# Attention sums of the first units out of the value products, key copies ahead of maxima, and first weight packs rounded on GpSimd

## The chip, the cores and the metric

The kernel runs on one core of a Trainium2 chip. The core has five engines with a queue each: TensorE (PE: matmuls, with weight loads listed apart as PEld), VectorE (DVE), ScalarE (ACT), GpSimd (POOL) and SyncE (SP), which here issues every DMA. Each engine runs its queue in program order and waits on semaphores for the others. The metric is the time of one execution in device microseconds (us), as the median of several runs; a profile shows one execution.

## The reference

Two stages, all in float32. First an attention over 4 batches of 8 heads, 768 positions and 64 numbers per head, in which a query sees the keys less than 16 positions away and 24 block summaries:

```python
k_sum = k.reshape(B, H, nb, 32, D).max(axis=3)
v_sum = v.reshape(B, H, nb, 32, D).mean(axis=3)
scores_l = np.where(|i - j| < 16, scale * q @ k.T, -1e9)
scores_s = scale * q @ k_sum.T + log(32)
a = exp(scores_all - max); a = a / (sum(a) + 1e-9)
attn = a @ concat(v, v_sum)
```

Then, on the 3072 rows x of 512 numbers that this gives: `out = ((x @ w_a) * (x @ w_b)) @ w_out`, with 1536 columns in the middle.

## The kernel before

**Work is cut in units.** A unit is 256 rows (two tiles of 128 queries), so there are 12. Per unit the second stage runs 12 items, one per 128 middle columns: 144 items. An item is 24 matmuls for `x @ w_a` and `x @ w_b` (line 959), a product on DVE (L979) between copies on ACT (L976, L981), a rest on DVE (L984) and 6 matmuls onto the output (L995). Float32 accuracy is had by parts: x and the weights are split into a rounded part and a rest, and three products are added. The split of x is a cast on ACT (L747) and a subtraction on DVE (L750).

**Weights** come in 36 loads (`load_part`, L255), two to a *pack*; `convert(j)` makes the parts of pack j = 0 to 17 by bit operations: scaling on ACT into PSUM bank c0 (L294), four steps on DVE (`step`, L309 to L333, with c1 between; three steps from pack 2 on, where ACT also writes the signs, L294 to S), then a rounding cast on ACT (L369) and a subtraction and an addition on POOL (L374, L380). Packs 0, 1 and 14 to 17 go in halves of 512 columns, the others in one piece of 1024. Loads of packs from 4 on wait for the pack four places earlier.

**Attention.** `first_keys` turns the six key chunks of batch 0 on PE (`turn`, L401), copies each out in two pieces on ACT (L460, L462) and takes block maxima on DVE (L470); POOL puts the summaries between the keys (L436). `first_attention` does units 0 and 1 (`u < FILL`), tiles 0 to 3, in this chain: the mask is laid into two PSUM banks by a matmul (L598), the queries are turned and scaled, the scores are added (L610), maxima on DVE (L643), exponentials on ACT with an accumulated sum (L655), then 1e-9 added, a reciprocal and a diagonal matrix of it on DVE (L664, L670, L677), a matmul of the exponentials with the diagonal that transposes and divides at once (L698), a copy on ACT (L710), the products with the values (L739) with the heads' dimensions on partitions, and the split of x. The means of the value blocks come from matmuls with `mean` (L852), copies on ACT (L864) and POOL (L870). Tiles 0 and 2 share buffers and banks o0, o1; tiles 1 and 3 share o2, o3. Later units (`attention`) divide on POOL (L685) and transpose on DVE (L725). Unit 2's two tiles use banks c0 and c1, which the conversion uses too: the second tile's scores stand behind pack 17's last use of them.

**The order** is planned by the class `Work`: every operation is added with an engine, a rank, an estimated duration and the keys that it reads and writes; `emit` then lets each engine take the operation with the lowest rank among those that the plan has ready. The ranks that matter here: CHAIN 0 for an item's copies and the scaling, FIRST 1 for unit 0 and keys, NEXT 2.3 for unit 1, CONVERT 2 + j/4 for pack j on DVE (0.5 less for its cast), SOON 5 for unit 2. The items of units 0 and 1 alternate, so that each new weight serves two items; from unit 2 on all weights are there.

Of the kernel before, what the change touches and what calls it, by code (L numbers as in the profile page):

```python
# [84 lines left out]
def attention_moe(  # L85
# [27 lines left out]
    SIGNS = 2  # L113
    AHEAD = (7, 9, 17)
# [64 lines left out]
    vbuf = [sb([P, H, D], f"vw{e}") for e in range(2)]  # L179
    for e in range(2):  # L180
        nc.vector.memset(vbuf[e], 0.0)
# [48 lines left out]
    CHAIN, FIRST, CONVERT, NEXT, SOON, PREP, LATER = 0, 1, 2, 2.3, 5, 5.5, 6  # L230
# [40 lines left out]
    def convert(j):  # L271
# [81 lines left out]
        for hs in spans:  # L353
# [13 lines left out]
            act(  # L367
                rank - 0.5, 0.25 + 0.37 * len(hs), f + rk, hi,
                lambda ms=ms, f8=f8: nc.scalar.copy(out=parted(0)[:, ms], in_=f8),  # L369
            )  # L370
# [73 lines left out]
    def first_keys():  # L444
        n = P // BLK
        for i in range(S // P):
# [7 lines left out]
            pe(FIRST, 0.85, [key], [bk], lambda bk=bk, x=x: turn(bank[bk], x))  # L454
            c0 = PER * i

            def put(lo, bk=bk, c0=c0):
                tr = bank[bk].rearrange("p (c x) -> p c x", x=P)
                if lo:
                    nc.scalar.copy(out=kT[:, :, c0 + 16 : c0 + WIN], in_=tr[:, :, : WIN - 16])  # L460
                else:
                    nc.scalar.copy(  # L462
                        out=kT[:, :, c0 + P : c0 + PER + 16], in_=tr[:, :, WIN - 16 :]
                    )
# [11 lines left out]
        for c in range(NP):  # L476
            work.add("-", 0, 0, 0, [f"ksi{i}" for i in range(6)], [f"ks{c}"], lambda: None)
            reads = [f"kT{x}{i}" for i in range(6) for x in "lh"]
            work.add("-", 0, 0, 0, reads, [f"kT{c}k"], lambda: None)
            summaries(FIRST, c)  # L480
# [93 lines left out]
    def load_values(b, t, vw, keys, rank):  # L574
# [3 lines left out]
        for i, (e, r0, lo, hi) in enumerate((  # L578
# [5 lines left out]
                rank, 2.1 * (hi - lo), 215, (), [keys[i]], vw[e][r0 : r0 + hi - lo],  # L584
# [3 lines left out]
    def scores(u, t, qT, qk, s, sk, banks, diag=None, lead=None):  # L588
        kind = 0 if t == 0 else 2 if t == S // P - 1 else 1
        rank = rank_of(u) + (0.2 * (t % G) if u < FILL else 0)  # L590
        m, mk = nml[t % 2], f"nml{t % 2}"


        masked = u < FILL

        def masks():
            for h in range(2):
                nc.tensor.matmul(  # L598
                    bank[banks[h]].rearrange("p (c x) -> p c x", x=P), ident,
                    mask[:, kind, None, :].broadcast_to([P, NP, P]), start=True, stop=False,  # L600
                )

        def fn():
            for c in range(NP):
                for h in range(2):
                    hs = slice(h * D, (h + 1) * D)
                    for e in range(2):
                        es = slice(e * QT, (e + 1) * QT)
                        c0 = PER * t + QT * e
                        nc.tensor.matmul(  # L610
                            bank[banks[h]][es, c * P : (c + 1) * P], qT[hs, c, es],
                            kT[hs, c, c0 : c0 + P],
                            start=not masked, stop=not masked or c == NP - 1,
                            tile_position=(h * D, e * QT),
                        )

        if masked:
            pe(rank + 0.1, 1.8, [], banks, masks)
        if lead is None:
            pe(-1, 1.2, [qk] + KT, banks, fn)  # L620
        else:

            def both():
                lead[2]()
                fn()

            pe(-1, 2.2, lead[0] + [qk] + KT, [lead[1], *banks], both)
# [446 lines left out]
```

## Time and profile before

| what | us |
|---|---|
| median of 3 runs | 705.59 (703.9 to 707.14) |
| the profiled execution, whole | 703.89 |
| its span from the first to the last instruction | 702.2 |
| mean granted clock of TensorE | 0.995 |

Lines of a page or view name an engine, a kernel line (L), what is written and read, and a count (x). An entry in brackets is the idle time of the engine before the instruction and what ended it. A timeline's first two columns are start and duration in us, and neighbours of one kind are merged into a row.

### The profile page before, as it was taken

To read this page: it belongs to the slowest core of one execution; us is meant where nothing else is said; L and a number is where in the kernel's file an instruction comes from. 1 tells how busy PE (TensorE), PEld (TensorE's weight loads), DVE (VectorE), ACT (ScalarE), POOL (GpSimd) and SP (SyncE) were. 2 spreads that over 40 slices of the span, in tenths; PEclk is the share of its full clock that TensorE was granted. 3 is DMA by queue.
4 is the path that set the end of the run, shared out by engine and by line. 5 is a ranking of instruction groups with operands and counts; after the bars stand their busy time and mean duration, and the time that the engine had idled before them with its cause. 6 is when DMAs were issued, how large, how long until landed. Compare 5 with 4: busy or idle time off the path is not lost.

```text
span 702.2 us, 15117 instructions
## 1 busy us (share of the span) xinstructions
PE 682.5 (97%) x6000; PEld 626.5 (89%) x6000; DVE 439.8 (63%) x992; ACT 271.2 (39%) x815; POOL 182.3 (26%) x220
## 2 busy tenths in 40 slices
PE   6889999999999999999999999999999999999997
PEld 3768998898999999999999999999999999999996
DVE  2899899897767777767665776762762662311221
ACT  2998787532424332333332323332331431211211
POOL 5269878652442440113110101110110110000000
PEclk9989999999999999999999999999999999999999
DMA  9989835165224245132210330310310100000000
GB/s 227 280 182 291 301 80 155 27 141 125 64 74 98 70 99 116 32 58 78 54 24 17 69 67 2 87 24 1 84 24 1 54 21 1 31 1 1 31 1 31
DMA packets 154943, 54.84 MB, mean 78 GB/s; under 512 B 132456, under 2 KB 147816, under 8 KB 154872
## 3 DMA queue, kind: packets, MB, share of 16 engines
q1 hardware_dynamic: 154872, 53.88, 32.0%
q8 instruction: 47, 0.77, 0.5%
q14 instruction: 24, 0.20, 0.1%
HBM read 47.12 MB, written 6.29 MB: 76 GB/s over the span
## 4 chain that ended last, share of the span: by engine, by line
PE 85%; DVE 7%; ACT 4%; DMA 2%; issue 1%; POOL 0%; SPq 0%; POOLq 0%; DVEq 0%; ACTq 0%
PE h L959 51%; PE o L995 27%; PE c L739 2%; PE c L610 2%; PE o L739 2%; DVE pt L725 1%; DMA raw<-in_moe_w_b_dram 1%; PE o L610 1%; ACT s L655 1%; DVE c L327 1%; ACT c L294 1%; ACT S L294 1%; DVE ksum L470 1%; PE o L598 1%; DVE gl L984 0%
## 5 line engine op out<-in xcount | busy, mean ns | idle before, releaser
L959 PEld LDWEIGHTS h<-x,w 128*128 128x128 f32 x3456 | 413.9, 188 | 10.8 <-DVE c L327 0.2
L959 PE MATMUL h<-x,w 128*128 128x256 f32 x3456 | 416.3, 277 | 0.0
L979 DVE TENSOR_TENSOR h<-h,g 128x256 f32<-128x256 f32 x144 | 62.0, 430 | 163.7 <-ACT g L976 162.4
L976 ACT COPY g<-h 128x256 f32<-128x256 f32 x144 | 53.7, 373 | 277.6 <-PE h L959 276.8
L995 PE MATMUL o<-w,gh 128*128 128x512 f32 x576 | 158.0, 396 | 1.9 <-ACT gh L981 1.9
L995 PEld LDWEIGHTS o<-w,gh 128*128 128x128 f32 x576 | 98.8, 188 | 19.5 <-ACT gh L981 2.7
L725 DVE STREAM_TRANSPOSE pt<-s 32x256 f32<-32x256 f32 x240 | 104.7, 436 | 8.3 <-POOL s L685 4.0
L685 POOL TENSOR_TENSOR s<-s,nml 128x512 f32<-128x512 f32 x40 | 41.7, 1042 | 243.1 <-DVE nml L670 241.5
L995 PE MATMUL o<-w,gl 128*128 128x512 f32 x288 | 89.7, 393 | 0.0
L655 ACT ACTIVATE s<-s,nml 128x128 f32<-128x128 f32 x160 | 62.5, 393 | 49.5 <-DVE nml L643 46.8
L984 DVE TENSOR_TENSOR gl<-h,gh 128x256 fp32r<-128x256 f32 x144 | 60.5, 420 | 29.7 <-ACT gh L981 28.2
L981 ACT CAST gh<-h 128x256 fp32r<-128x256 f32 x144 | 53.5, 372 | 62.9 <-DVE h L979 62.6
L995 PEld LDWEIGHTS o<-w,gl 128*128 128x128 f32 x288 | 53.9, 188 | 11.7
L540 POOL TENSOR_TENSOR S<-S 96x512 f32<-96x512 f32 (+3 forms) x48 | 33.5, 698 | 49.6 <-DMA S<-in_v_dram 39.8
L655 ACT ACTIVATION_READ_ACCUMULATOR s<-s,nml 128x1 f32 x160 | 30.3, 190 | 0.0
L664 DVE TENSOR_SCALAR nml<-nml 128x4 f32<-128x4 f32 x40 | 11.5, 287 | 30.0 <-ACT s L655 30.0
L374 POOL TENSOR_TENSOR space<-space,w 128x1024 f32<-128x1024 f32 (+1 forms) x13 | 26.8, 2058 | 11.8 <-ACT w L369 10.9
L380 POOL TENSOR_TENSOR w<-space 128x1024 fp32r<-128x1024 f32 (+1 forms) x13 | 26.8, 2064 | 1.0
L294 ACT ACTIVATE S<-raw 128x1024 f16<-128x1024 f32 (+1 forms) x20 | 23.1, 1153 | 6.5 <-DVE S L309 4.6
L643 DVE TENSOR_REDUCE nml<-s 128x4 f32<-128x512 f32 x40 | 25.2, 667 | 0.0
L294 ACT ACTIVATE c<-raw 128x512 f32<-128x512 f32 x36 | 23.2, 645 | 4.0 <-DVE space L320 1.5
L436 POOL COPY kT<-ksum 128x144 f32<-128x144 f32 x16 | 4.7, 307 | 61.0 <-DVE ksum L518 55.0
(104 smaller groups left out, 478.0 us busy)
## 6 DMA issues: line engine op xcount, KB each, us to landing
raw<-in_moe_w_a_dram SPq DMA_DIRECT2D x12, 512.0 KB
raw<-in_moe_w_b_dram SPq DMA_DIRECT2D x12, 512.0 KB
raw<-in_moe_w_out_dram SPq DMA_DIRECT2D x12, 512.0 KB
out_dram<-S SPq DMA_DIRECT2D x24, 256.0 KB
qin<-in_q_dram SPq DMA_DIRECT2D x160, 32.0 KB
S<-in_v_dram SPq DMA_DIRECT2D x24, 192.0 KB
vw<-in_v_dram SPq DMA_DIRECT2D x18, 192.0 KB
kin<-in_k_dram SPq DMA_DIRECT2D x24, 100.0 KB
```

The lines of the kernel that those rows point to most:

```text
L294: nc.scalar.mul(out=zhalf[:, lo:hi] if out is None else out, in_=high.bitcast(F32), mul=2.0**-112)
L540: lambda: nc.gpsimd.tensor_tensor(out=out, in0=i0, in1=i1, op=ALU.add),
L655: lambda h=h, c=c, sums=sums: nc.scalar.activation(s[h][:, c, :], x[h][:, c, :], AF.Exp, bias=m[:, 0, h, c : c + 1], scale=1.0, accum_out= ...
L685: lambda h=h, r=r: nc.gpsimd.tensor_tensor(out=s[h], in0=s[h], in1=r[:, :, None].broadcast_to([P, NP, P]), op=ALU.mult,),
L725: lambda js=js, qs=qs: nc.vector.transpose(out=pv[js, :, qs], in_=sv[qs, :, js]),
L739: nc.tensor.matmul(ps[h * D : (h + 1) * D, c, es], vw[e][:, 2 * c + h, :], d[:, h, c, es], start=True, stop=True, tile_position=(0, h * D),)
L959: nc.tensor.matmul(ps, w[:, c, part, :], x[xpart][:, c, :], start=(i == 0), stop=(i == n - 1))
L976: act(CHAIN, 0.38, [hk], [gk], lambda: nc.scalar.copy(out=g, in_=pa))
L979: lambda: nc.vector.tensor_tensor(out=pa, in0=pb, in1=g, op=ALU.mult),
L981: act(CHAIN, 0.41, [hk], [ghk], lambda: nc.scalar.copy(out=gh, in_=pa))
L984: lambda: nc.vector.tensor_tensor(out=gl, in0=pa, in1=gh.bitcast(F32), op=ALU.subtract),
L995: nc.tensor.matmul(bank[ok[j]], (gh if first else gl)[:, js], w[:, :, part, :], start=(f == 0 and first and part == 0), stop=(f == NF - 1 ...
```

## The change

Four things change together.

1. In units 0 and 1 the sums of the exponentials come out of the value products. The value buffers get a 65th column of ones per head, and the products are formed with the queries on partitions (`weigh`), so that column 64 holds the sum. The exponentials have no accumulator, they are transposed by the identity, the division comes after the products, and the result is turned back on PE. The second set of value buffers moves in part to the upper half of S1.
2. The halves of the value rows for the block means are added on POOL, and one mean matmul per chunk is left instead of two.
3. In `first_keys` both copies stand ahead of the maximum, which waits for them. The mask matmuls wait for the first key turn and are one per bank.
4. Packs 0 to 3 are rounded by POOL instead of ACT (`FIRSTS = 4`). NEXT goes from 2.3 to 1.5, and the first two weight loads from ranks 8 and 9 to 5 and 5.5, ahead of unit 0's queries (6 and 7).

For units 2 to 11 the same operations are written in other functions.

```diff
+    vbuf = [sb([P, H, D + 1], f"vw{e}") for e in range(2)]
     for e in range(2):
-        nc.vector.memset(vbuf[e], 0.0)
+        nc.vector.memset(vbuf[e][:, :, :D], 0.0)
+        nc.vector.memset(vbuf[e][:, :, D:], 1.0)
...
-    CHAIN, FIRST, CONVERT, NEXT, SOON, PREP, LATER = 0, 1, 2, 2.3, 5, 5.5, 6
+    CHAIN, FIRST, CONVERT, NEXT, SOON, PREP, LATER = 0, 1, 2, 1.5, 5, 5.5, 6
...
+            if j < FIRSTS:
+                pool(
+                    rank - 0.5, 0.1 + 0.55 * len(hs), f + rk, hi,
+                    lambda ms=ms, f8=f8: nc.gpsimd.tensor_copy(out=parted(0)[:, ms], in_=f8),
+                )
+            else:
...
-            act(FIRST, 0.43, [bk], [f"kTl{i}"], lambda put=put: put(True))
-            act(FIRST, 0.33, [bk], [f"kTh{i}"], lambda put=put: put(False))
+            act(FIRST, 0.75, [bk], [f"kT{i}"], put)
             dve(
-                FIRST, 0.6, [bk], [f"ksi{i}"],
+                FIRST, 0.6, [bk, f"kT{i}"], [f"ksi{i}"],
...
+    def early_scores(u, t, qT, qk, s, sk, banks):
...
+        for h in range(2):
+            pe(
+                rank + 0.1, 0.9, ["first"], [banks[h]],
+                lambda h=h: nc.tensor.matmul(
+                    x[h], ident, mask[:, kind, None, :].broadcast_to([P, NP, P]),
+                    start=True, stop=False,
+                ),
+            )
+        pe(-1, 1.2, [*qk] + KT, banks, lambda: dots(t, qT, banks, False))
...
+                act(
+                    rank, 0.2, [f"{mk}m{h}", banks[h]], [sk[h]],
+                    lambda h=h, c=c: nc.scalar.activation(
+                        s[h][:, c, :], x[h][:, c, :], AF.Exp, bias=m[:, 0, h, c : c + 1]
+                    ),
+                )
...
+    def early_values(u, t, s, sk, banks, pt, vw, vk):
...
+        def turned(h):
+            for c in range(NP):
+                nc.tensor.transpose(bank[banks[h]][:, c * P : (c + 1) * P], s[h][:, c, :], ident)
...
+        def weigh(j):
+            for i in range(NP):
+                g = NP * j + i
+                for e in range(2):
+                    es = slice(e * QT, (e + 1) * QT)
+                    nc.tensor.matmul(
+                        ps[j][es, i, :], d[:, g % 2, g // 2, es], vw[e][:, g, :],
+                        start=True, stop=True, tile_position=(0, e * QT),
+                    )
+
+        for j in range(2):
+            pe(-1, 0.55, dk[0] + dk[1] + vk, [banks[j]], lambda j=j: weigh(j))
+        for j in range(2):
+            l = m[:, 1, j, :]
+            dve(
+                rank, 0.15, [banks[j]], [f"{mk}l"],
+                lambda j=j, l=l: nc.vector.tensor_scalar(
+                    out=l, in0=ps[j][:, :, D], scalar1=1e-9, scalar2=None, op0=ALU.add
+                ),
+            )
+            dve(rank, 0.15, [], [f"{mk}l"], lambda l=l: nc.vector.reciprocal(out=l, in_=l))
+            dve(
+                rank, 0.4, [banks[j], f"{mk}l"], [sk[0]],
+                lambda j=j, l=l: nc.vector.tensor_tensor(
+                    out=xn[:, j * 256 : (j + 1) * 256].rearrange("p (g d) -> p g d", d=D),
+                    in0=ps[j][:, :, :D], in1=l[:, :, None].broadcast_to([P, NP, D]), op=ALU.mult,
+                ),
+            )
+        pe(-1, 0.6, [sk[0]], [banks[1]], lambda: turn(bank[banks[1]], xn))
+        split(u, t, banks[1])
...
+            pool(
+                FIRST, 0.7, [], [key],
+                lambda x=x: nc.gpsimd.tensor_tensor(
+                    out=x[:, :, :D], in0=x[:, :, :D], in1=x[:, :, D:], op=ALU.add
+                ),
+            )
+            pe(FIRST + 0.5, 0.5, [key, mk], ["h0"], lambda n=n: means(n))
...
-    for i, rank in enumerate((8, 9, 17, 17.5, 19, 20)):
+    for i, rank in enumerate((5, 5.5, 17, 17.5, 19, 20)):
```

More of the change, by code (lines that the diff above doesn't have):

```diff
@@ L477, in first_keys @@
             work.add("-", 0, 0, 0, [f"ksi{i}" for i in range(6)], [f"ks{c}"], lambda: None)
-            reads = [f"kT{x}{i}" for i in range(6) for x in "lh"]
-            work.add("-", 0, 0, 0, reads, [f"kT{c}k"], lambda: None)
+            work.add("-", 0, 0, 0, [f"kT{i}" for i in range(6)], [f"kT{c}k"], lambda: None)
             summaries(FIRST, c)
@@ L583, in load_values, with scores @@
             load(
-                rank, 2.1 * (hi - lo), 215, (), [keys[i]], vw[e][r0 : r0 + hi - lo],
+                rank, 2.1 * (hi - lo), 215, (), [keys[i]], vw[e][r0 : r0 + hi - lo, :, :D],
                 heads(v[b, :, lo:hi, :]),
             )
-    def scores(u, t, qT, qk, s, sk, banks, diag=None, lead=None):
+    def scores(u, t, lead=None):
         kind = 0 if t == 0 else 2 if t == S // P - 1 else 1
-        rank = rank_of(u) + (0.2 * (t % G) if u < FILL else 0)
+        rank = rank_of(u)
         m, mk = nml[t % 2], f"nml{t % 2}"
[L594 to L618, printed above, removed]
+        banks = ["c0", "c1"] if u == FILL or t % G == 0 else ["o2", "o3"]
         if lead is None:
-            pe(-1, 1.2, [qk] + KT, banks, fn)
+            pe(-1, 1.2, ["qT"] + KT, banks, lambda: dots(t, qTs, banks, True))
         else:
@@ L691, in transposes @@
[L691 to L714 removed]
+                rank, 0.15, [], lk,
@@ new lines, in scores @@
+                lambda l=l: nc.vector.tensor_scalar(
+                    out=l, in0=l, scalar1=1e-9, scalar2=None, op0=ALU.add
+                ),
+            )
+            dve(rank, 0.15, [], lk, lambda l=l: nc.vector.reciprocal(out=l, in_=l))
+            pool(
+                rank, 1.05, lk, [SK[h]],
+                lambda h=h, l=l: nc.gpsimd.tensor_tensor(
+                    out=s0[h], in0=s0[h], in1=l[:, :, None].broadcast_to([P, NP, P]), op=ALU.mult
+                ),
+            )
@@ L730, in products, with split @@
+    def split(u, t, bk):
         rank = rank_of(u)
         ps = bank[bk].rearrange("p (c x) -> p c x", x=P)
-        d, dk = pt or PD
+        hi, lo = (y[:, :, P * (t % G) : P * (t % G + 1)] for y in xs[u % 2])
+        xk = f"x{u % 2}.{t % G}"
+        act(rank, 0.6, [bk], [xk + "h"], lambda: nc.scalar.copy(out=hi, in_=ps))
+        dve(
+            rank, 0.6, [bk, xk + "h"], [xk + "l"],
+            lambda: nc.vector.tensor_tensor(out=lo, in0=ps, in1=hi.bitcast(F32), op=ALU.subtract),
+        )
@@ L734, in fn, with products @@
+    def products(u, t, bk):
+        ps = bank[bk].rearrange("p (c x) -> p c x", x=P)
         def fn():
@@ L924, in attention @@
             begin(0)
-            turned(0)
+            transposes(u)
             yield
@@ L943, in attention @@
                 bring(i)
-                turned(i)
+                transposes(u)
                 lead.append(products(*end(i)))
         if u == NU - 1:
-            reads, bk, fn, split = lead.pop()
+            reads, bk, fn, then = lead.pop()
             pe(-1, 1.1, reads, [bk], fn)
-            split()
+            then()
         yield
```

244 lines of the change are left out of this document (114 added, 130 removed).

## The prediction

> **What bounds the kernel now.** The page comes first: its busy line.
>
> ```profile
> PE 682.5 (97%) x6000; PEld 626.5 (89%) x6000; DVE 439.8 (63%) x992; ACT 271.2 (39%) x815; POOL 182.3 (26%) x220
> ```
>
> TensorE (PE) is busy 97% of 702.2 us. An average hides where time is lost, so the next view cuts the span into stretches; each row gives the stretch, its length, busy time and instructions of PE, weight loads, VectorE (DVE), ScalarE (ACT) and GpSimd (POOL), then granted clock, DMA share and GB/s.
>
> ```profile
> core 0: us, PE busy (x) PEld busy (x) DVE busy (x) ACT busy (x) POOL busy (x), PEclk, DMA share, GB/s
> ...
> 17.50:27.00 9.50, 8.20 (x99) 7.08 (x100) 7.89 (x17) 8.24 (x35) 0.91 (x4) 1.00 1.16 249
> 27.00:40.00 13.00, 12.29 (x163) 8.72 (x165) 12.39 (x22) 11.96 (x28) 7.75 (x8) 1.00 0.98 243
> 40.00:50.00 10.00, 7.05 (x58) 6.46 (x51) 9.60 (x22) 9.77 (x34) 5.42 (x4) 0.85 0.81 191
> 50.00:62.50 12.50, 11.14 (x112) 9.67 (x111) 11.73 (x21) 11.28 (x20) 12.05 (x6) 0.85 1.06 295
> 62.50:86.00 23.50, 23.50 (x202) 22.02 (x201) 20.68 (x38) 18.33 (x29) 20.56 (x10) 1.00 0.94 315
> 86.00:110.00 24.00, 24.00 (x175) 22.51 (x176) 23.51 (x42) 19.77 (x42) 18.84 (x9) 1.00 0.39 81
> 110.00:130.00 20.00, 18.13 (x130) 16.64 (x129) 19.21 (x38) 12.29 (x27) 13.69 (x10) 1.00 0.35 109
> 130.00:139.00 9.00, 9.00 (x65) 8.30 (x63) 7.87 (x14) 4.85 (x11) 8.20 (x7) 1.00 0.17 39
> 139.00:161.30 22.30, 21.92 (x225) 19.60 (x224) 20.49 (x49) 8.82 (x31) 13.37 (x18) 1.00 0.61 127
> 161.30:702.20 540.90, 536.62 (x4753) 499.29 (x4751) 301.37 (x727) 160.72 (x557) 72.36 (x98) 1.00 0.20 46
> ```
>
> From 161.3 us on PE is busy 536.62 of 540.9 us with work that the change does not touch. What the change can move is the time at which that part begins. From 62.5 to 161.3 us PE idles only 0 + 0 + 1.87 + 0 + 0.38 = 2.25 us. Before 62.5 it computes just two of the 144 items, so its other work there is attention and waiting. Its own rows mark the places:
>
> ```profile
> 111.95 1.20 PE L995 MATMUL o<-w,gh 128*128 128x512 f32 x4 [1.16 <-ACT gh L981]
> ...
> 129.43 1.20 PE L995 MATMUL o<-w,gh 128*128 128x512 f32 x4 [0.71 <-ACT gh L981]
> ...
> 157.30 1.15 PE L739 MATMUL c<-pt,vw 128*64 128x64 f32 x32 [0.38 <-DVE x L750]
> ...
> 161.26 5.62 PE L959 MATMUL h<-x,w 128*128 128x256 f32 x48
> ```
>
> The two waits on gh (1.16 and 0.71 us) are most of the 2.25, and at 161.26 the first item of the third unit begins, after the third unit's attention. So the date to forecast is the one that now stands at 161.26.
>
> What sets that date? In the rows of 17.5 to 161.3 us DVE is busy 7.89 + 12.39 + 9.60 + 11.73 + 20.68 + 23.51 + 19.21 + 7.87 + 20.49 = 133.4 of 143.8 us, 93%. PE's busy time contains matmuls that queue; DVE's does not. DVE carries the whole conversion of the weights (18 packs), the vector part of the attention of units 0 to 2 and two operations per item, and the third unit's second tile can only start when the last pack has left banks c0 and c1. I therefore read the stretch as **bound by DVE**, with ACT beside it only up to 62.5 us: there ACT has 8.24 + 11.96 + 9.77 + 11.28 = 41.3 of 45 us, DVE 41.6. PE has waiting work: the second unit's x is done only here,
>
> ```profile
> 63.20 0.68 DVE L750 TENSOR_TENSOR x<-o,x 128x512 fp32r<-128x512 f32 x1
> ```
>
> at 63.88, and that is what keeps the dense part from starting before 62.5.
>
> **The change part by part.** *Keys.* Six key chunks pass in turn through ACT, DVE and ACT again; the last of them:
>
> ```profile
> 8.02 1.76 PE L401 MATMUL c<-ident,space 128*128 128x128 f32 x8
> ...
> 9.62 1.04 PE L401 MATMUL o<-ident,space 128*128 128x128 f32 x8
> ...
> 15.20 0.69 DVE L470 TENSOR_REDUCE ksum<-c 128x16 f32<-128x512 f32 x1 [0.71 <-ACT kT L460]
> ...
> 15.92 0.32 ACT L462 COPY kT<-c 128x192 f32<-128x192 f32 x1 [0.76 <-DVE ksum L470]
> ...
> 16.60 0.69 DVE L470 TENSOR_REDUCE ksum<-c 128x16 f32<-128x512 f32 x1 [0.71 <-ACT kT L460]
> ...
> 17.36 1.05 POOL L436 COPY kT<-ksum 128x144 f32<-128x144 f32 x4 [5.92 <-DVE ksum L470]
> ...
> 18.71 0.69 DVE L315 TENSOR_SCALAR space<-c 128x512 int32<-128x512 int32 x1 [1.42 <-ACT c L294]
> ```
>
> ACT L462 waits 0.76 us for DVE, and a chunk costs 16.60 - 15.20 = 1.40 us: a maximum of 0.69 and two copies, 0.71 together. In the new form both copies stand ahead of the maximum, the next chunk's copies run beside it in another bank, and the pace falls to DVE's 0.69, or to the arrival of the data. For that the DMA rate, in 40 slices of 0.9 us:
>
> ```profile
> GB/s 0 0 96 289 235 219 216 218 217 218 218 221 234 288 346 348 331 292 290 290 290 290 270 200 196 212 184 127 341 360 372 260 199 202 337 405 369 355 349 333
> ```
>
> Summed, 1.57 MB (all keys) have come by 9.0 us. One turn (0.9, half of the eight at 8.02), two copies and a maximum behind that end at about 11.5 us instead of 17.29. The 5.8 us are not worth 5.8 us, because of the loads.
>
> The masks' matmuls now wait for the first key turn; the key turns queue beside them on PE, and they have until the dots to be done, so I price that at nothing (at worst a maximum ends later, which the queries' arrival below hides by 2 us).
>
> *Loads.* The first two weight parts go ahead of the first queries:
>
> ```profile
> 8.55 1.11 SPq L255 DMA_DIRECT2D raw<-in_moe_w_a_dram  x1
> ...
> 21.82 1.98 SPq L255 DMA_DIRECT2D raw<-in_moe_w_out_dram  x1
> ...
> 30.24 0.69 DVE L333 SCALAR_TENSOR_TENSOR space<-raw,c 128x512 f32<-128x512 uint32 x1
> ...
> 31.11 0.69 DVE L315 TENSOR_SCALAR space<-c 128x512 int32<-128x512 int32 x1 [0.19 <-ACT c L294]
> ```
>
> The weights (1.05 MB, at the 288 to 348 of the slices in which they travel now) then come by about 12 us, not 15, and the queries (0.52 MB) by 14.5, not 11.6: the first tile's queries land at about 13.3, and its dots, which now follow the copies that end at 18.41, move to about 15.5. The order is the same on SP's queue as on the wire. The bytes ahead of pack 1's first part (issued at 21.82) stay the same, so its arrival stays: 6.1 MB are summed at 27.1 us, the scaling on ACT (0.65) makes it 27.8. So DVE can begin pack 1 at best at 27.8, where it now begins at 31.11, directly behind pack 0's last step at 30.24. Between 12 and 27.8 it has room for pack 0 (8 x 0.69 = 5.5), four maxima (2.8) and tile 0's new division (1.6, next part). Left for after 27.8 are tile 1's division and both splits, 1.6 + 1.4; now 1.4 are left at 31.11. Lead: 3.3 - 1.6 = 1.7, up to 2.4 if tile 0's split (0.7) is done by then, as 21.1 us for the last values allows: 21.1 + POOL's add 0.65, the mean and two copies at 0.6 each 1.75 + products 1.15, division 1.6, turn 0.55, cast 0.6 and subtraction 0.7 = 28.1. I take **2.2 us**.
>
> *Sums by ones.* The groups up to 62.7 us (busy, mean ns):
>
> ```profile
> L380 POOL TENSOR_TENSOR w<-space 128x512 fp32r<-128x512 f32 x4 | 5.2, 1289 | 0.3
> ...
> L655 ACT ACTIVATION_READ_ACCUMULATOR space<-o,nml 128x1 f32 x16 | 2.8, 177 | 0.0
> ...
> L677 DVE TENSOR_TENSOR pt<-ident,o 128x512 f32<-128x512 f32 x4 | 2.7, 687 | 0.2
> L677 DVE TENSOR_TENSOR space<-ident,o 128x512 f32<-128x512 f32 x4 | 2.7, 686 | 0.1
> L655 ACT ACTIVATION_READ_ACCUMULATOR s<-o,nml 128x1 f32 x16 | 2.7, 168 | 0.0
> ...
> L369 ACT CAST w<-space 128x512 fp32r<-128x512 f32 x4 | 2.4, 613 | 0.0
> ...
> L369 ACT CAST w<-space 128x1024 fp32r<-128x1024 f32 x2 | 2.1, 1066 | 0.0
> ...
> L664 DVE TENSOR_SCALAR o<-o 128x4 f32<-128x4 f32 x8 | 1.3, 165 | 0.2
> ...
> L870 POOL COPY space<-vw 32x512 f32<-32x512 f32 x2 | 1.2, 609 | 11.7 <-ACT vw L864 11.7
> ...
> L979 DVE TENSOR_TENSOR h<-h,g 128x256 f32<-128x256 f32 x2 | 0.9, 428 | 0.2 <-ACT g L976 0.2
> ```
>
> Gone are 8 diagonals on DVE (L677: 2.7 + 2.7 = 5.5) and 32 accumulator reads on ACT (2.8 + 2.7 = 5.5). In their place come 8 products of 128x256 out of PSUM. No row has that form with a broadcast operand; the bounds are L664's 165 ns and L677's 687, and I take L979's 428, which has the shape: 3.4. L664 and the reciprocal stay, 8 each. Net on DVE -2.1 us (-4.2 to 0), half of it in tiles 0 and 1 and contained above: **1.0 us** for unit 1. The division needs per tile 2 x (0.17 + 0.19 + 0.43) = 1.6 as used above.
>
> *TensorE.* Transposing by identity instead of the diagonal's matmul halves the passes; the products with queries on partitions are again 32 small passes, and a turn back is added:
>
> ```profile
> L739 PE MATMUL o<-space,space 128*64 128x64 f32 x32 | 1.2, 225 | 0.0
> ```
>
> a product set in the present form costs 1.15 (the new form, 64 columns of weights and 65 moving, has no row: half to double of it), a turn at best 0.53 (four transposes at the 130 ns of 9.62), at worst 0.88 (at 8.02). PE is not short before 62.5 us; this is cost nothing, and if PE became short it would be 4 x 0.9 = 3.6 us on the units' chains. The halved mean matmuls and POOL's six adds (0.65 each, half of L380's 1289 ns for 512) lie beside the arrival of values.
>
> *POOL rounds packs 0 to 3.* ACT loses 4 x 0.61 + 2 x 1.07 = 4.6 us (the second shape at 1.06 also when it reads S). POOL gains four of 512, for which L870's 609 ns stand, and two of 1024, doubled: 4.9 us (bounds per 512: 0.31, the 144-wide copies of 17.36, to L380's 1.29 with two inputs). With the reads, ACT sheds about 10 of its 41.3 us. DVE's idle time from 27 to 62.5 is 0.61 + 0.40 + 0.77 = 1.8 us, while ACT was 92% busy; between none and all of it I take half, **0.9 us**.
>
> *Rank of the second unit.* It now goes ahead of packs 0 and 1. Tile 0 takes 12.6 us from its dots at 15.5 to its x at 28.1; for tiles 2 and 3, which overlap and start behind tiles 0 and 1, I allow 16 to 20 more. So unit 1's x comes near 46 us instead of 63.9, and DVE's work is only reordered. The dense part can begin early, then waits for weights: their pace is DVE's. Lead of PE beyond DVE's is worth the slack that stands at the end: after 157.30 products, cast and subtraction (1.15 + 0.6 + 0.7) make x ready at 159.8, PE takes it up at 161.26. Of 1.4 I take **0.9 us**.
>
> Sum: 2.2 + 1.0 + 0.9 + 0.9 = **5.0 us**. The profiled execution took 703.89 us, 1.7 below the median 705.59; so 698.9 by the profile, **700.6** by the median.
>
> **Rivals.** *POOL takes over.* In 50 to 62.5 us POOL is busy 12.05 of 12.5, in 62.5 to 86 20.56 of 23.5: its two operations per pack already run back to back. If its 4.9 us fall into that string, packs from 4 on come no earlier, the 5.0 are eaten: 705.5. Against it: packs 0 and 1 are rounded before 40 us, where POOL is half empty, and after 86 it has 5.2 us of air. [...] Chance 0.13.
>
> *The clock falls.* In 40 to 62.5 us, where PE idles between attention steps, the granted clock is 0.85, and eight transposes took 1.76 at 8.02 but 1.04 at 9.62. The new early part has more transposes and fewer matmuls. If it ran at that slow pace, a tile's PE steps (about 4.6) would grow by two thirds, 3 us, and on the two tiles in a row 6, with the first items late as well: gain near 1, 704.5. But it decides only where unit 1's x then comes too late, and 46 + 6 is still ahead of 63.9; chance 0.06. [...]
>
> *DVE stands in line* (slower). Each engine runs in the order planned with estimated durations (0.6 us for DVE's 0.69, 340 KB/us for weights that come at 290 to 348). Tile 0's division stands at rank 1, ahead of packs, and waits for all values (21.1 us) plus sums. If the order puts it ahead of pack 0's steps, these 5.5 us stand behind a wait on DVE and packs slide; from 5.0 us of such idle on the gain is gone, at 10 (two tiles) 710.6. For it: DVE's steps behind the values rise from two splits to two divisions and two splits. Against it: pack 0 would be ready some 8 us before. Chance 0.11.
>
> *More than the sum.* DVE still idles 2.82 + 0.49 + 0.79 + 1.13 + 1.81 = 7.0 us between 62.5 and 161.3. If a PE well ahead (unit 1's x 17 us sooner, as above) lets three quarters of it go, the gain is 5.0 + 5.3: 695.3. Chance 0.18.
>
> **How the numbers follow.** The forecast's case has 0.52, spreading over 697.5 to 703.5 (division 0 to 4.2, lead 1.7 to 2.4, slack 0 to 1.4, idle 0 to 1.8). A measurement tells about 0.5%, 3.5 us: faster means under 702.1, slower over 709.1. Faster: 0.7 of 0.52, and 0.18: 0.54. Same: the rest, 0.16 + 0.13 + 0.06 = 0.35. Slower 0.11. The range leaves out the slower rival and the lower part of the last: 694.5 to 706.5.
>
> **What would show it.** Last key maximum ending near 11.5 us; first dots near 15.5; no DVE gap over 1 us behind 27; pack 1 begun near 28; unit 1's x near 46; dense PE from about 50 with waits for weights between; the third unit's first item near 156 instead of 161.26, and the tail after it of equal length. I am wrong if that tail changes, if POOL's operations run without gap to the last pack (POOL takes over), or if DVE idles more than 4 us between 12 and 62 behind the first values.

## The result and the profile after

| | before | after |
|---|---|---|
| median of 4 runs, us | 705.71 (703.90 to 707.14) | 712.51 (711.25 to 713.51) |
| profiled execution, us | 703.89 | 711.73 |
| its span, us | 702.2 | 709.9 |
| start of the third unit's first item, us | 161.26 | 159.88 |
| from there to the end of the span, us | 540.9 | 550.0 |

The changed kernel takes 1.0100 of the time before (95% interval 1.0082 to 1.0117). It was forecast 5.0 us faster; it is 6.8 us slower in these runs, and 4.9 slower in a later repetition of both kernels (a_again below). The table splits the error: the early part, which the change rewrites, ends 1.4 us sooner and not 5.0, and the late part, in which no operation changed, is 9.1 us longer. Ratios leave out runs over 1.5% above the fastest of their kernel; medians, ranges and counts are of all runs, since the scatter is itself in question.

The page's busy line and the stretches of the changed kernel, with the columns of the prediction's view (length, then PE, weight loads, DVE, ACT, POOL, granted clock, DMA share, GB/s) and the last cut at the third unit's first item:

```profile
PE 688.4 (97%) x5972; PEld 630.3 (89%) x5972; DVE 435.9 (61%) x994; ACT 264.1 (37%) x777; POOL 190.8 (27%) x234
```

```profile
core 0: us, PE busy (x) PEld busy (x) DVE busy (x) ACT busy (x) POOL busy (x), PEclk, DMA share, GB/s
17.50:27.00 9.50, 7.86 (x111) 6.37 (x104) 3.93 (x11) 6.56 (x20) 8.29 (x12) 1.00 0.98 247
27.00:40.00 13.00, 9.70 (x96) 6.65 (x95) 9.49 (x20) 8.05 (x18) 2.01 (x3) 0.87 0.96 257
40.00:50.00 10.00, 6.84 (x89) 5.08 (x88) 9.66 (x17) 8.66 (x18) 9.65 (x9) 0.91 0.96 241
50.00:62.50 12.50, 12.19 (x101) 11.12 (x102) 10.83 (x26) 8.06 (x15) 10.25 (x5) 0.80 1.10 330
62.50:86.00 23.50, 23.50 (x191) 21.43 (x190) 21.85 (x40) 19.49 (x30) 22.19 (x11) 1.00 0.61 222
86.00:110.00 24.00, 22.92 (x165) 21.04 (x164) 23.38 (x43) 20.06 (x42) 19.97 (x10) 1.00 0.54 128
110.00:130.00 20.00, 20.00 (x146) 18.63 (x144) 19.09 (x40) 12.07 (x28) 14.41 (x10) 1.00 0.32 106
130.00:139.00 9.00, 9.00 (x89) 8.06 (x88) 7.44 (x14) 5.40 (x11) 7.80 (x7) 1.00 0.23 54
139.00:159.90 20.90, 20.81 (x193) 18.88 (x192) 20.21 (x49) 7.70 (x28) 12.21 (x17) 1.00 0.62 132
159.90:709.90 550.00, 544.57 (x4753) 505.57 (x4751) 299.94 (x727) 160.75 (x557) 72.42 (x98) 1.00 0.20 45
```

DVE is busy for 125.9 us from 17.5 to 159.9, against 133.4 to 161.3 before. All of this difference lies ahead of 62.5 us (33.9 against 41.6); behind it DVE has 92.0 us against 91.8. Most of it is work that moved: ahead of 17.5 us DVE is now busy for 10.1 us instead of 5.1, and over the whole span it has 3.9 us less (435.9 against 439.8). PE idles only 1.2 us between 62.5 and 159.9. In the last row the matmul count is that of before (4753), the granted clock is 1.00 as before, and yet it lasts 9.1 us longer.

**Where the late part's 9.1 us are.** First a stretch of the changed kernel's PE timeline, then the same time before:

```profile
429.90 2.99 PE L1004 MATMUL h<-x,w 128*128 128x256 f32 x24
432.72 1.10 PE L1040 MATMUL o<-w,gh 128*128 128x512 f32 x4
433.66 0.62 PE L1040 MATMUL o<-w,gl 128*128 128x512 f32 x2
434.12 2.99 PE L1004 MATMUL h<-x,w 128*128 128x256 f32 x24
```

```profile
429.65 2.91 PE L959 MATMUL h<-x,w 128*128 128x256 f32 x24
432.39 1.08 PE L995 MATMUL o<-w,gh 128*128 128x512 f32 x4
433.31 0.62 PE L995 MATMUL o<-w,gl 128*128 128x512 f32 x2
433.77 2.91 PE L959 MATMUL h<-x,w 128*128 128x256 f32 x24
```

An item, the same 30 matmuls, takes 434.12 - 429.90 = 4.22 us instead of 4.12, with no wait in either. Taking the starts of single matmuls from the trace, the 24 of a chain follow each other at 113.3 ns (mean of the later ones) in the quick form and at 117.8 ns in the slow one. So TensorE has **two paces** for one instruction stream. The trace of before has 143 of 144 chains at the quick pace; that of after has 82 at the slow one: items 0, 10 and 11, 18 to 21, 26, and 43 to 116. The last stretch begins behind a wait of PE and ends at 594:

```profile
197.33 0.34 PE L789 MATMUL c<-pt,vw 128*64 128x64 f32 x4 [0.44 <-DMA vw<-S]
198.09 1.03 PE L789 MATMUL c<-pt,vw 128*64 128x64 f32 x28 [0.43 <-DMA vw<-S]
...
245.77 1.04 PE L789 MATMUL o<-pt,vw 128*64 128x64 f32 x28 [0.40 <-DVE pt L678]
...
250.64 5.82 PE L1004 MATMUL h<-x,w 128*128 128x256 f32 x48
...
594.06 5.63 PE L1004 MATMUL h<-x,w 128*128 128x256 f32 x48
...
600.90 2.91 PE L1004 MATMUL h<-x,w 128*128 128x256 f32 x24
```

In the late part 75 slow chains at 0.10 us make 7.5 us and the three waits on unit 3's products 1.3 us: 8.8 of the 9.1. Before, the late part has no such wait of PE. PE's own order there differs by one swap near 170 us only, but the inputs stand later against it: PE comes to the first products at 196.9 us instead of 198.09, SP issues their value sums at 194.92 instead of 194.70, and at 244.4 DVE has three transpositions left instead of two.

**Where the early part's gain stayed.** Timeline rows of the changed kernel, of DVE, SP's queue, ACT and PE:

```profile
10.50 1.28 DVE L479 TENSOR_REDUCE ksum<-c 128x16 f32<-128x512 f32 x2
...
25.51 0.16 DVE L754 TENSOR_SCALAR nml<-o 128x4 f32<-128x4 f32 x1 [5.07 <-PE o L743]
...
25.92 0.42 DVE L761 TENSOR_TENSOR s<-o,nml 128x256 f32<-128x256 f32 x1
...
27.72 0.69 DVE L318 TENSOR_SCALAR space<-c 128x512 int32<-128x512 int32 x1 [0.64 <-ACT c L297]
...
32.45 0.16 DVE L754 TENSOR_SCALAR nml<-o 128x4 f32<-128x4 f32 x1 [1.32 <-PE o L743]
...
36.01 1.29 DVE L702 TENSOR_REDUCE nml<-o 128x4 f32<-128x512 f32 x2 [1.27 <-PE o L660]
...
39.13 0.69 DVE L336 SCALAR_TENSOR_TENSOR space<-raw,c 128x512 f32<-128x512 uint32 x1
...
45.75 1.28 DVE L702 TENSOR_REDUCE nml<-o 128x4 f32<-128x512 f32 x2
...
59.15 0.69 DVE L777 TENSOR_TENSOR x<-o,x 128x512 fp32r<-128x512 f32 x1 [0.22 <-ACT x L774]
```

```profile
29.76 7.26 SPq L229 DMA_DIRECT2D qin<-in_q_dram  x9
...
38.61 3.47 SPq L229 DMA_DIRECT2D qin<-in_q_dram  x7
42.87 1.55 SPq L229 DMA_DIRECT2D vw<-in_v_dram  x3
```

```profile
47.83 1.39 ACT L297 ACTIVATE S<-raw 128x1024 f16<-128x1024 f32 x1
```

```profile
14.35 2.01 PE L410 MATMUL h<-ident,space 128*128 128x128 f32 x8 [2.58 <-DMA space<-in_q_dram]
16.28 1.63 PE L660 MATMUL o<-kT,qT 64*64 64x128 f32 x32
...
46.10 0.30 PE L743 MATMUL o<-vw,pt 128*64 128x65 f32 x2 [0.95 <-DMA vw<-in_v_dram]
47.45 1.39 PE L743 MATMUL o<-vw,pt 128*64 128x65 f32 x30 [1.05 <-DMA vw<-in_v_dram]
50.06 1.97 PE L722 MATMUL o<-ident,space 128*128 128x128 f32 x8 [1.23 <-ACT space L710]
...
57.90 0.60 PE L410 MATMUL o<-ident,space 128*128 128x128 f32 x4
58.25 1.18 PE L1040 MATMUL o<-w,gh 128*128 128x512 f32 x4
59.27 0.62 PE L1040 MATMUL o<-w,gl 128*128 128x512 f32 x2
59.73 3.07 PE L1004 MATMUL h<-x,w 128*128 128x256 f32 x24
```

And of the kernel before, the end of pack 1 on DVE and the start of item 2 on PE (items are numbered here as their chains come on PE, so item 2 is the third):

```profile
37.01 0.69 DVE L333 SCALAR_TENSOR_TENSOR space<-raw,c 128x512 f32<-128x512 uint32 x1
```

```profile
56.00 1.08 PE L995 MATMUL o<-w,gh 128*128 128x512 f32 x4
...
59.78 1.17 PE L995 MATMUL o<-w,gh 128*128 128x512 f32 x4
60.89 1.15 PE L739 MATMUL o<-space,space 128*64 128x64 f32 x32
61.97 0.74 PE L995 MATMUL o<-w,gl 128*128 128x512 f32 x2
62.54 1.65 PE L959 MATMUL h<-x,w 128*128 128x256 f32 x13
```

Pack 1 starts at 27.72 as forecast, but its last step ends at 39.82, where it ended at 37.70 before: two divisions and tile 2's maxima stand in between, with 1.32 and 1.27 us of waiting. Unit 1's x comes at 59.84, not 46. For its first tile (tile 2) the values are late: SP issues them at 42.87, behind 16 query transfers for unit 2, and PE waits 0.95 and 1.05 us for them. The x that ends last is the second tile's (tile 3), and it stands behind other work: its maxima start on DVE at 45.75, behind conversion steps, tile 1's split and item 0's operations, which run without a gap from 37.22; on ACT two scalings (47.83 to 49.7) part its exponentials; its eight transposes take 1.97 us; and its turn back, at 57.90, stands on PE behind item 1's chain. The dense part starts 2.8 us sooner (item 2 at 59.73 for 62.54), of which 1.4 go to item 1's six downward matmuls, which stood ahead of item 2 before and now stand behind it.

### The profile page after: what moved, and what is told of

Same layout as the page of the kernel before. It is cut to its first block, busy times and chain, and to the rows that moved or that the text cites. A ratio compares the mean times of both kernels' runs of the same rounds, so it can differ in the third digit from the quotient of the medians.

```text
span 709.9 us, 15057 instructions
## 1 busy us (share of the span) xinstructions
PE 688.4 (97%) x5972; PEld 630.3 (89%) x5972; DVE 435.9 (61%) x994; ACT 264.1 (37%) x777; POOL 190.8 (27%) x234
## 4 chain that ended last, share of the span: by engine, by line
PE 78%; DVE 7%; SPq 5%; DMA 4%; ACT 3%; issue 2%; POOL 1%; DVEq 0%; ACTq 0%; POOLq 0%
PE h L1004 47%; PE o L1040 24%; SPq L229 4%; PE c L789 2%; SPq L258 1%; PE o L660 1%; PE o L789 1%; DVE pt L678 1%; PE c L660 1%; DVE c L330 1%; DMA raw<-in_moe_w_out_dram 1%; DMA raw<-in_moe_w_b_dram 1%; ACT S L297 1%; DMA space<-in_q_dram 1%; DVE space L336 1%
## 5 line engine op out<-in xcount | busy, mean ns | idle before, releaser
L1004 PEld LDWEIGHTS h<-x,w 128*128 128x128 f32 x3456 | 420.0, 189 | 12.2 <-DVE x L777 1.3
L1004 PE MATMUL h<-x,w 128*128 128x256 f32 x3456 | 423.2, 279 | 1.2 <-DVE x L777 0.9
L548 POOL TENSOR_TENSOR S<-S 96x512 f32<-96x512 f32 (+3 forms) x48 | 33.6, 701 | 41.3 <-DMA S<-in_v_dram 31.6
L640 DVE TENSOR_SCALAR nml<-nml 128x4 f32<-128x4 f32 x40 | 8.8, 219 | 29.2 <-ACT s L632 29.2
```

What stands on the lines that cost most here:

```text
L548: lambda: nc.gpsimd.tensor_tensor(out=out, in0=i0, in1=i1, op=ALU.add),
L1004: nc.tensor.matmul(ps, w[:, c, part, :], x[xpart][:, c, :], start=(i == 0), stop=(i == n - 1))
```

## The experiments

Theory first: the late time comes from the slow pace, which TensorE falls into by the timing of what enters it (**rhythm**). First rival: the value buffers' 65 columns move every later buffer by 64 bytes, and operands at these places are read more slowly (**addresses**). For each run stand the median, all that matters of the single runs, and the slow chains of its one profile.

**a_pad** and **b_pad.** After the line of the value buffers:

```diff
+    sb([P, 240], "pad")     # a_pad, in the changed kernel; b_pad: [P, 16] in the kernel before
```

> The changed kernel with one unused buffer of 960 bytes behind the value buffers, so that all later buffers stand 1024 bytes from where they stood before the change, instead of 64; the order is untouched. Theory 'addresses' (the 64 bytes slow the item matmuls): the item matmuls go back to 113 to 114 ns all the way, about 704 us. Theory 'rhythm' (TensorE falls into one of two paces by the timing of what enters its queue): nothing that the addresses decide, 82 of 144 items at the 118 ns pace as now, 711 to 714 us.

> The kernel before with one unused buffer of 64 bytes behind the value buffers: later buffers stand where the change puts them. Addresses: many items at 118 ns, 712 us. Rhythm: as before, 704 to 707 us, at most one or two items at 118 ns.

a_pad: 704.93 us, 704.09 to 707.99 in 10 runs, 1.0009 of before (0.9993 to 1.0025); 15 slow chains, the longest stretches 14 to 19 and 43 to 46. b_pad: 704.62, 703.82 to 705.70 in 10 runs, no slow chain. The pad takes the late loss away from the changed kernel, but the same shift does nothing to the kernel before: addresses alone don't make it slow.

**a_rank** and **a_first0.** One part of the change undone in each:

```diff
-    CHAIN, FIRST, CONVERT, NEXT, SOON, PREP, LATER = 0, 1, 2, 1.5, 5, 5.5, 6
+    CHAIN, FIRST, CONVERT, NEXT, SOON, PREP, LATER = 0, 1, 2, 2.3, 5, 5.5, 6
-    for i, rank in enumerate((5, 5.5, 17, 17.5, 19, 20)):
+    for i, rank in enumerate((8, 9, 17, 17.5, 19, 20)):
...
-    FIRSTS = 4
+    FIRSTS = 0
```

> The changed kernel with NEXT at 2.3 and the first loads at ranks 8 and 9 again: another order in the first 60 us, the same operations. If the date of the third unit's first item is set by these ranks it moves by more than 1 us from 159.9; I expect 158 to 163. Rhythm: the share of items at 118 ns changes with the timing, in either direction, and total minus that date moves with it by 0.1 us per item. Addresses: the share stays near 82 of 144.

> The changed kernel with ScalarE rounding packs 0 to 3 again. If POOL's extra 4.9 us hold up the packs, the third unit's first item comes earlier than 159.9, by up to 3 us; if not, it comes within 1 us or later, since ScalarE carries 4.6 us more. Rhythm: the share of slow items changes with the timing; addresses: it stays near 82.

a_rank: 705.12, 706.57, and four from 713.68 to 715.80; a_first0: 702.29, and three from 713.48 to 718.87. The profiles, both of low runs, have 11 and 2 slow chains and none behind item 26; the third unit's first item stands at 162.72 and 159.18, less apart than it varies between profiles of one order (below). One kernel, with one set of addresses, gives runs over 11 us apart (702.29 and 713.48 in a_first0); that the high ones are in the slow pace is read from their times, since they have no trace. With either part undone the high runs are still there, so neither is needed for them.

**a_again, a_pad_again, a_free, b_stall.** The changed kernel and the padded one once more on one chip; the changed kernel with unit 3's products planned later; and the kernel before with one late step held up:

```diff
-                    load(97, 49.0, 100, sums, [VK[3 + e]], vbuf[e][r0 : r0 + NS, :, :D], vsums[b])
+                    load(97, 49.0, 10, sums, [VK[3 + e]], vbuf[e][r0 : r0 + NS, :, :D], vsums[b])
-                    rank, 0.45, SK, [f"pt{i}{j}"],
+                    rank, 0.9 if u == FILL + 1 else 0.45, SK, [f"pt{i}{j}"],
...
+                twice = u == FILL + 1 and t % G == 1 and (i, j) == (3, 3)    # b_stall
-                    lambda js=js, qs=qs: nc.vector.transpose(out=pv[js, :, qs], in_=sv[qs, :, js]),
+                    lambda js=js, qs=qs, n=1 + twice: [
+                        nc.vector.transpose(out=pv[js, :, qs], in_=sv[qs, :, js])
+                        for _ in range(n)
+                    ],
```

> The changed kernel as it is, once more, on the chip on which the padded copy runs too. Theory 'addresses' (the place of the buffers sets TensorE's pace): 712.5 in all runs, as in the first four, beside 705 for the padded copy. Theory 'rhythm' (a wait of TensorE in the late part throws it into the slower of two paces, 117.75 instead of 113.3 ns per item matmul, and it stays there for a number of chains that differs from run to run): runs scatter between about 702 and 716, the two kernels overlap, and the trace shows the slow chains beginning right behind a wait of TensorE (such as the 0.40 us on pt at 245.77).

> The changed kernel with 960 more bytes behind the value buffers, once more. 'Addresses': 704.9 in all runs again, all apart from the unpadded copy's. 'Rhythm': the same scatter as the unpadded copy; the ten runs at 704 to 708 were short stays in the slow pace, and the medians of the two kernels differ by no more than their scatter.

> The changed kernel with two planned durations raised, the last transpositions of unit 3 (0.45 to 0.9) and the load of the value sums (rate 100 to 10), so that the planner puts TensorE's products of unit 3 later and TensorE waits neither at 197 nor at 245 us. The order up to the third unit stays. 'Rhythm by waits': no wait of TensorE behind 165 us, no slow chains behind the last wait, about 702 to 703.5 in nearly all runs (profile: the third unit's first item at 160 to 163, then 540.9). If waits have nothing to do with it: slow chains all the same, and a scatter up to 712 or more.

> The kernel before with one addition: the last of the ten transpositions of unit 3's second tile is issued twice (0.43 us of VectorE), so that TensorE waits some 0.4 us for it at 245 us, as the changed kernel does. Everything else keeps its order. 'Rhythm by waits': slow chains begin at item 43 in this trace or runs scatter, up to some 10 us above 705 in part of them; with 100 chains in the slow pace the run would be 10 us longer. If a wait alone does nothing: 705.3, the wait itself, and all chains at 113.3 ns.

a_again: 710.06, 701.70 to 714.06 in 12 runs, four of them up to 703.76 and seven from 709.70 (without the highest runs, as above, 1.0012 of before, 0.9980 to 1.0044). a_pad_again: 705.45, none above 707.35 in 11 runs. So the scatter of the changed kernel is real, and the pad ends it on the same chip: 7 of 12 runs against none of 11 above 708. Both profiles enter the slow pace at item 43; the padded one leaves it at 47, the unpadded one at 117, exactly as the first profile of the changed kernel. The padded one entered with no wait of PE between chains 42 and 43. a_free was a miss for the idea that a wait is needed: its waits moved to 216 and 219.5 us instead of going, and its long stretch, 63 to 116, began without one; 707.25 to 714.81. In b_stall the hold-up was small, the products took 1.32 us instead of 1.18 with no wait listed:

```profile
247.36 1.32 PE L743 MATMUL o<-pt,vw 128*64 128x64 f32 x32
```

Behind it the chains 43 to 46 were slow, and runs lay at 703.79 to 709.05 (median 705.98), against 703.79 to 708.01 of the kernel before beside them: no difference clear of noise. The slow pace also comes up in the order of before, here behind the late step, but it left again within four chains.

**b_stall_pad, a_first0_pad.** The two edits combined with the pads (64 and 960 bytes):

> The kernel before with both: the repeated transposition of b_stall, so that TensorE is held up at unit 3's second tile, and 64 bytes behind the value buffers, so that all later buffers stand where the changed kernel has them. Theory 'wait enters, addresses keep': the wait sends the item chains into the slow pace from item 43 and, as in the changed kernel, they leave it only at item 117 (74 chains x 24 x 4.4 ns = 7.8 us), so part of the runs come at 711 to 714, others at 704 to 706, and the slow ones' share is like the changed kernel's (8 of 12 above 706). Theory 'waits alone': as b_stall, left at item 47, 703.8 to 709. Theory 'something else of the change keeps it slow': as b_stall too.

> The changed kernel with the first packs rounded on ScalarE as before, and 960 more bytes behind the value buffers. 'Wait enters, addresses keep': no run above 708, nearly all at 701.5 to 703.5, as the unpadded one's single undisturbed run (702.29); the third unit's first item near 159.5. If the place of the buffers has no part in it: again a share of the runs at 713 to 719.

b_stall_pad: 704.51, 703.73 to 705.75 in 12 runs, 3 slow chains (24 to 26). So a held-up step and the shift do not make the long stay. a_first0_pad: 707.33, 705.08 to 710.20 in 12 runs, 12 slow chains: the 713 to 719 are gone with the pad, but four runs lie above 708 where none was expected, and 702.29 didn't come back; its third unit starts at 163.5, not 159.2.

**b_wide_stall, a_pad16, a_kick, a_one.** The last four on the pace: the buffers' form in the order of before; another pad; and one matmul issued twice, 18 times or once (in b_wide_stall, the copy that fills these buffers is written for the wider heads too):

```diff
-    vbuf = [sb([P, H, D], f"vw{e}") for e in range(2)]
+    vbuf = [sb([P, H, D + 1], f"vw{e}")[:, :, :D] for e in range(2)]     # b_wide_stall, on b_stall
...
+    sb([P, 16], "pad")                                                   # a_pad16
...
         def hidden():
+            if u > FILL and f in (0, 6):       # a_kick; a_one: u == FILL + 1 and f == 6
+                nc.tensor.matmul(
+                    pa, weight(f, "a")[:, 0, 0, :], x[0][:, 0, :], start=True, stop=True
+                )
```

> The kernel before with the value buffers laid out 65 columns a head as in the changed kernel (all later buffers 64 bytes on, too) and the repeated transposition of b_stall; the order of the work is that of before. If the buffers' form keeps the slow pace: part of the runs at 709 to 714 and slow chains over dozens of items. If it takes the changed kernel's order: 703.7 to 709 as b_stall and b_stall_pad, slow stretches of four chains at most.

> The changed kernel with 64 more bytes behind the value buffers (128 in all against before; a_pad has 1024). If only the particular place of the changed kernel's buffers locks the rhythm, or if any shift re-rolls it: like a_pad, 703.5 to 708, the late slow stretch left at item 47. If whole multiples of a larger line are needed: scatter up to 714 with a slow stretch from item 43 to 117.

> The changed kernel, buffers where they are, with 18 more matmuls in the late part: items 0 and 6 of units 3 to 11 issue the first matmul of their chain twice (the second begins the sum anew). Their own price is 18 x 0.115 = 2.1 us. Theory 'a rhythm that is kept until something shifts it': slow stretches end at one of the next repeated matmuls, the high runs at 710 to 714 go, and all runs lie at 704 to 707, 2.1 above the changed kernel's undisturbed 701.7 to 703.8. If a single matmul shifts nothing: the same scatter as before plus 2.1, 704 to 716.

> The changed kernel, buffers where they are, with one more matmul in the whole program: item 6 of unit 3 (item 42 of 144) issues its first matmul twice, for 0.12 us. If the high runs come from the one place at which both traces of the changed kernel entered the slow pace for 74 chains (item 43): no run above 708 any more, median 702 to 704, below the kernel before. If the rhythm is entered at other places as well (a repeated matmul at the other items was needed): part of the runs still at 709 to 714.

a_pad16: 705.58, 704.41 to 706.82 in 12 runs, no slow chain behind item 26: 128 bytes in all against before do it as the 1024 of a_pad do, so no multiple of more than 128 is needed. With a_pad and a_pad_again that is 33 runs of the padded changed kernel without one above 708, against 11 of 16 of the unpadded. b_wide_stall: 703.90 to 705.19 in 11 runs and one of 712.65. Its profile, of a run of 704.91, has no slow chain; the high run has no trace, so whether the changed buffers bring a long stay in the order of before is not shown. a_kick: 706.78, 704.53 to 708.43 in 12 runs, that is 702.4 to 706.3 without the 2.1 us that the 18 matmuls are reckoned at: the high runs are gone, as expected, if up to 708.43 and not 707. Its profile has one slow chain, item 26, so it doesn't show a repeated matmul ending a slow stretch.

a_one, with one repeated matmul alone: 706.81, six runs from 703.13 to 705.93, one of 707.68 and five from 710.71 to 713.62. Its profile entered at item 33, in the first chain behind the waits on vw, and left at 117, and the added matmul stands in the middle of this stretch:

```profile
244.51 0.28 PE L1018 MATMUL h<-x,w 128*128 128x256 f32 x1
244.63 2.99 PE L1004 MATMUL h<-x,w 128*128 128x256 f32 x24
```

The chains ahead of it and behind it are slow (2.99 us each). So the one repeated matmul that a trace shows inside a slow stretch did not end it, against the theory that a_kick was made for. Nor is there a single door: the slow pace is entered at several places (items 33, 43 and 63), and all four long stays that a trace shows end at item 117.

**What leaving the slow pace looks like.** The starts of matmuls around item 47, as differences in ns, from the traces of after (stays slow) and a_pad (turns quick). The 64 small matmuls of attention ahead agree within 2 ns. Then the 12 downward matmuls and the chain:

```
after  339 231 237 232 231 226 229 232 226 229 232 226 | 118 117 119 117 118 118 118 117 118 118
a_pad  341 232 232 226 229 231 226 229 232 226 229 231 | 117 117 118 122 118 114 113 113 114 113
```

The downward matmuls run in a cycle of three, 232, 226 and 229 ns, in both; the two traces enter the chain at different points of the cycle, and after a step of 122 ns in the fourth place the padded one runs at 113 to 114. In after the same happens at the head of item 117: steps of 118, 117, 117, 123 and 118 ns, then 113 to 114.

**b_dve.** Is DVE the bound of the early part? On the kernel before:

```diff
+                again = n == 2 and h == 0 and 6 <= j < 14
-                dve(rank, 0.6, reads, writes, lambda n=n, h=h: step(n, h))
+                dve(
+                    rank, 0.6, reads, writes,
+                    lambda n=n, h=h, again=again: [step(n, h) for _ in range(1 + again)],
+                )
```

> The kernel before with more work for VectorE: one conversion step of packs 6 to 13 is issued twice, 8 x 0.69 = 5.5 us in the stretch from about 65 to 125 us; all else keeps its order. The prediction's theory (VectorE bounds 17.5 to 161.3 us): the third unit's first item moves from 161.3 by 3.5 to 5.5 us, 709 to 711. Rival (TensorE bounds from the start of item 2 at 62.85, and this start sets the date): it moves by under 1 us and the time stays within 705 to 706.5; TensorE's waits behind 62.5 grow by as little.

708.92 us against 705.15, ratio 1.0057 (1.0038 to 1.0076): 3.8 of the 5.5 us came through, and the third unit's first item stood at 166.59. From item 2 to there it took 102.4 us instead of 98.6 to 98.7 in five profiles of the order of before. So added work on DVE costs all but some 1.8 us here: by that much DVE falls short of being what bounds this stretch.

**a_vals.** The padded kernel, with unit 2's queries planned behind unit 1's values:

```diff
-            qk += blocks(98, f"qin.{c}", qin[:, c, :], q, b, c, r * CH)
+            qk += blocks(98, f"qin.{c}", qin[:, c, :], q, b, c, r * CH, VK[:1] if u == FILL else ())
```

> The padded changed kernel, with the queries' loads of the third unit planned behind the values of the second unit's first tile, so that SP's queue issues these values ahead of 16 query transfers. Theory 'TensorE bounds from item 2 on, and item 2 waits for the second unit's x': x moves from about 60 to 63 (four profiles of the changed order) to about 57, item 2 with it, and the third unit's first item to about 159.5, not further, since TensorE then waits for weights or for unit 2's attention; 702 to 703.5. Prediction's theory (VectorE bounds, the date of the second unit's x has no price): within 0.5 us of the padded kernel's 704.9 to 705.5.

708.11 us, 707.42 to 709.02 in 6 runs: slower than a_pad. SP issued the values at 31.29 instead of 42.87, and x of tile 2 was done at 49.6 instead of 56.7 to 59.4. But weights then came later, and ACT, in its planned order, stood before them with the copies of item 1 behind:

```profile
57.25 1.34 ACT L298 ACTIVATE S<-raw 128x1024 f16<-128x1024 f32 x1 [4.45 <-DMA raw<-in_moe_w_out_dram]
...
59.02 0.36 ACT L1022 COPY g<-h 128x256 f32<-128x256 f32 x1
```

```profile
61.21 1.22 PE L1041 MATMUL o<-w,gh 128*128 128x512 f32 x2 [5.21 <-ACT gh L1027]
```

So unit 1's second tile was later than ever, at 65.5. SP's order was a cause of the first tile's late x and not of the second's, which here stood behind the arrival of the weights. Both expected times were missed; but item 2 stood at 64.62 and the third unit's first item at 164.62, again 100.0 us behind it.

## Why the prediction was wrong

**The step that failed first** is "PE is busy 536.62 of 540.9 us with work that the change does not touch". The instructions are the same, their pace is not. So the term "the tail after it of equal length" was put at nothing and came to 9.1 us: 7.5 us of slow chains and 1.3 us of new waits. They turn the sign: the changed kernel's lowest runs (four of a_again, 701.70 to 703.76) lie below all 29 runs of before beside them (703.79 to 708.01). These four have no trace, so that they were free of long stays is read from their times; lowest against lowest, the change would be worth an estimated 2 us without the slow pace. None of the rivals had this; the prediction did name a tail of other length as what would make it wrong.

**The bound.** "The date to forecast is the one that now stands at 161.26" was the right place, and "bound by DVE" was half right. b_dve shows that added DVE work lengthens the stretch from item 2 to that date by 3.7 of 5.5 us. But from item 2 to the third unit's first item the order of before takes 98.6 to 98.7 us in five profiles, and that of after 99.9 to 100.5 in eight (1.4 of it for item 1's downward matmuls), while item 2 itself starts anywhere from 59.3 to 63.1 in these eight. The end follows the beginning one to one, so the date was set ahead of item 2. That doesn't tell PE from DVE behind it, because DVE's steps shift along: the 21st step of line L336, which ends a pack's conversion (L337 where the pad adds a line), starts at 89.53 with item 2 at 59.35 (a_kick) and at 93.27 with item 2 at 63.06 (a_pad). What it does show is that time saved on DVE ahead of item 2 counts only if item 2 starts sooner. On average it started 2.2 us sooner (61.3 for 63.5), of which the 1.4 us of item 1's matmuls are no gain; what else DVE had less of turned into idle time there. Over the same profiles the third unit's first item moved from 162.2 on average (161.1 to 163.5) to 161.5 (159.3 to 163.2): a gain of about 0.7 us, within the scatter. The prediction's reading of before was off here too: the dense part's first chain runs without a pause from 62.54, while unit 1's x is done at 63.88, so it doesn't wait for that x; it stands on PE behind unit 1's products (60.89).

**Term by term.** Keys: the last maximum ended at 11.78 (11.5 forecast), as worked out. First dots at 16.28 (15.5), the queries landed later. Pack 1 at 27.72 (27.8); but the **lead of 2.2** counted only what stands ahead of pack 1 and not what is put between its steps, and at its last step it was a lag of 2.1. **Sums by ones, 1.0**: the multiply took 0.42 (0.428 taken), and what DVE saved became idle time, as above. **0.9 for ACT's relief**: ACT fell from 41.3 to 31.3 us in 17.5 to 62.5 as counted, and DVE's idle time there rose from 3.4 to 11.1. **0.9 of slack** needed unit 1's x near 46; it came at 59.84, 28.7 us behind tile 0's x (31.13) and not 16 to 20, because the price of a reordered unit was worked out from the steps of its chain, without what stands between them in the queues: SP's 16 query transfers for tile 2; conversion steps on DVE, scalings on ACT and item 1's chain on PE for tile 3.

**Rivals.** "DVE stands in line" happened, with 5.07 us of idle at 25.51, but with pack 0 done ahead (its last step at 16.91) and pack 1 not there before 27.7 it cost little: that the time came out slower, as this rival had it, is luck. POOL did not become the bound. The clock fell to 0.87, 0.91 and 0.80 in the stretches from 27 to 62.5, and eight transposes took 1.97 us at 50.06, near the prediction's slow value of 1.76, with a granted clock of 0.50 over them (50.06 to 52.03); whether that clock goes with the transposes or with PE's waits beside them is not shown. *More than the sum* did not occur: DVE's idle time behind 62.5 fell from 7.0 to 5.4 us, and not by three quarters.

**What stays open.** Shown are the two paces, that they make the late time in the traces, and that the changed kernel's high runs (11 of 16) are gone with a pad of 64 or 960 bytes (0 of 33) and with 18 repeated matmuls (12 of 12 up to 708.43). Not shown is which part of the change makes long stays so frequent (the waits on unit 3's products are a candidate, but a_free and a_pad_again entered without one), why the 18 matmuls help where a_one's did not, nor how the buffers' places act on the pace. No version of the changed kernel beats the kernel before by its median.

## What to carry to other kernels

A stretch in which no instruction changes can still change its time (540.9 and 550.0 us here): compare an item's start-to-start time in both traces before explaining anything else, and repeat both kernels, since four runs showed one of two groups here. An engine at 93% beside another at 98% is not "the bound" to be relieved; ask by how much, and test it by adding work to it, which is one line. When a step is moved forward, list what stands between its steps, in SP's queue as in the engines'.

## What the runs showed of the hardware that had not been expected

TensorE runs the same chain of 24 matmuls of 256 columns at 113.3 or at 117.8 ns each, both at a granted clock of 1.00, with no wait in the trace: the slow pace is 4% above the quick one. TensorE keeps the slow pace over up to 84 chains with rows of other matmuls between (393 us in a_one); in the late part of the changed kernel's first profile all four changes of pace (at items 26, 27, 43 and 117) lie where attention matmuls stand between two chains, while a_free left at item 38 without any. The places of buffers have a say: 64 bytes more, and no run of 12 had a time of the long stays (a_pad16, 706.82 at most). And the start of the third unit differs by up to 4 us between executions of one order (159.3 to 163.2, with pads and changes behind it among them), more than what the change gains there.
